# One part of four modes per weight transfer, and a 64-column block-diagonal product, in a spectral mixing kernel

## The chip, the core and the metric

The kernel runs on one core of a Trainium2 chip. The metric is device time in microseconds (us) of one execution; the numbers of the profile come from one profiled execution of its own.

## What is computed

Linear attention with the feature map elu + 1 gives `x` (8 batches, 576 positions, 512 columns). A real Fourier transform over the positions keeps 64 modes; each mode has its own complex 512 x 512 weight. The inverse transform is added to `x`, and a channel product with a rectifier follows. Cut to what matters:

```python
q_p, k_p = phi(q), phi(k)                         # phi = elu + 1
kv = einsum('bhsd,bhse->bhde', k_p, v)
x  = einsum('bhsd,bhde->bhse', q_p, kv) / (einsum('bhsd,bhd->bhs', q_p, k_p.sum(2))[..., None] + 1e-6)
X  = rfft(x, axis=1);  Xr, Xi = real(X[:, :64]), imag(X[:, :64])
Yr = einsum('bmd,mde->bme', Xr, w_r) - einsum('bmd,mde->bme', Xi, w_i)
Yi = einsum('bmd,mde->bme', Xr, w_i) + einsum('bmd,mde->bme', Xi, w_r)
u  = x + irfft(Yr + 1j * Yi)
out = u + maximum(u @ w_ch, 0)                    # float32
```

The weights `w_r` and `w_i` are 64 x 512 x 512 in float32 each, 134 MB together; a GpSimd DMA turns them into bfloat16 on the way.

## The kernel before

**Attention stage (to about 110 us).** Batch by batch: loads of q, k and v, features, the sums `kv`, the rows of `x`, the forward transform as matmuls against a table, and `place_x`, which spreads the transformed values over the 128 partitions in the order of the weights' rows (`xt_c`). The loads of the first weights are issued between (`w_next`), five pairs ahead.

**Weight stage (about 110 to 387 us).** A block `p` holds the weights of two modes, `2p` and `2p + 1`, both parts: tile `w[p]` is 128 partitions x 16 x 512. `w_load` (line 109) issues two transfers per block, one per part, each to every second partition: 64 rows of 16 KB. Five blocks are loaded ahead into five buffers; from then on two buffers turn over (`W_KEEP = 2`), so the load for block `p + 2` waits for the product of block `p`. Block 31 (`w_load_last`) comes in eight pieces, as its second mode is the last thing to arrive.

`mode_pair(p)` takes the block's weights, runs the product (line 502), copies the next block's values into a block-diagonal buffer on VectorE (`set_diagonal`, line 512), evacuates the sums (`evacuate`, on VectorE for even blocks at line 517, on ScalarE for odd ones at line 519), does pieces of other work, sums the column groups with `picks` (line 525), and does more other work. The product is 16 matmuls with 32 columns of weights (two modes, two parts, eight batches) against 512 columns of `w`; `tile_position` puts four of them on four column groups of the array. Two block-diagonal buffers `xz` take turns.

The other work (`work_slot`) is a list whose items were shared out over the blocks by hand: from block 5 on the rows of attention in float32 (lines 775 to 788, with the constant `kv_diag`, a memset at line 663), from block 15 on the fold of the early modes and the channel product (lines 802 to 852, after `YE_T`, line 550), from block 27 on the late modes (`YL`, line 635, then `z` and `yp`, lines 864 to 875, and `yb`, line 883). `keep_warm` (line 489) adds matmuls whose result nobody uses: 5 after blocks 18 to 22, 7, 10, 12 and 2 after blocks 27 to 30, and 3 inside block 30.

The last block's second mode is taken piece by piece as it lands (line 589); then come the last transposes, additions and stores (387 to 417 us).

Every engine works through its own instructions in the order of the program; `pin` keeps that order. All weight transfers are issued by GpSimd and run on one queue.

Of the kernel before, what the change touches and what calls it, by code (L numbers as in the profile page):

```python
# [20 lines left out]
def _dft_consts(S: int, NM: int):  # L21

    m = np.arange(NM)
    s_cols = np.concatenate([4 * np.arange(128) + jj for jj in range(4)] + [512 + np.arange(NP)])
    s_rows = np.concatenate([s_cols, s_cols[512:]]).reshape(5, 128).T
    ang = 2.0 * np.pi * s_rows[:, :, None] * m / S
    by_parity = np.concatenate([m[0::2], m[1::2]])
    fwd = np.concatenate([np.cos(ang)[:, :, by_parity], -np.sin(ang)[:, :, by_parity]], axis=2)

    return fwd.astype(np.float16)  # L30
# [3 lines left out]
def kernel(  # L34
# [20 lines left out]
    NMP = NM // 2  # L55
    XDC = 2 * B * NMP
# [18 lines left out]
    pick_sb = const.tile([128, 32], F16, name="pick_sb")  # L75
# [4 lines left out]

    xt_c = xpool.tile([128, NDW * XDC], BF16, name="xt_c")
    xt_v = xt_c.rearrange("p (c t b m) -> p c t b m", c=NDW, t=2, b=B)

    def xt_cols(dc: int, kk: int, n: int):

        dc = (dc // NDC * 2 + kk % 2) * NDC + dc % NDC
        c0 = dc * XDC + kk // 2
        return xt_c[:, c0 : c0 + (n - 1) * NMP + 1 : NMP]

# [14 lines left out]
    def w_load(p: int, half: int, pool, tag: str, bufs: int):  # L104
        if half == 0:
            w_in[p] = pool.tile([128, NDW, D], BF16, tag=tag, bufs=bufs, name=f"w{p}")
        two = (moe_w_r, moe_w_i)[half][2 * p : 2 * p + 2]
        pin(
            nc.gpsimd.dma_start(  # L109
                out=w_in[p][half::2], in_=two.rearrange("g (r dc) e -> (g r) dc e", dc=NDW)  # L110
            )
        )
# [24 lines left out]
    pending = [(p, half) for p in range(n_keep + n_pre) for half in range(2)]  # L137

    def w_next():
        p, half = pending.pop(0)  # L140
        pool, tag, bufs = (wpool, "w", W_KEEP) if p < n_keep else (wpre, "wp", W_PRE)
        w_load(p, half, pool, tag, bufs)
# [217 lines left out]
    place = sA.tile([128, 4, 66], BF16, name="place")  # L360
    place_l = sA.tile([128, 2, 130], BF16, name="place_l")
    nc.vector.memset(place, 0.0)
    nc.vector.memset(place_l, 0.0)

    def make_place():
        for i in range(4):
            pin(nc.vector.tensor_copy(out=place[:, i, 1:65:2], in_=id16[:, i::4]))
        for i in range(2):
            pin(nc.vector.tensor_copy(out=place_l[:, i, 1:129:2], in_=id16[:, i::2]))
        pin(nc.vector.tensor_copy(out=pick_sb, in_=id16[:, 0:32]))  # L370
        for quad in range(1, 4):
            pin(
                nc.vector.tensor_tensor(
                    out=pick_sb, in0=pick_sb, in1=id16[:, quad * 32 : quad * 32 + 32], op=ALU.add
                )
            )

# [3 lines left out]
    def place_x(b):  # L381

        x = xsp.pop(b).rearrange("p t c m -> p c t m")
        ps = psA.tile([128, 4, NDC, 2, NMP], F32, tag="big", bufs=3, name=f"xp{b}")
        for i in range(4):
            for o, ts in PARTS:
                for g in range(2):
                    pin(
                        nc.tensor.matmul(  # L389
                            ps[HALVES[g], i, :, :, 0 : NMP - 1],  # L390
                            place[:, i, 1 - o : 65 - o],
                            x[:, :, ts, g * NMP : g * NMP + NMP - 1],
                            start=(o == 0), stop=(o == 1), skip_group_check=True,
                        )
                    )
        for i in range(2):
            for g in range(2):
                for o, ts in PARTS:
                    pin(
                        nc.tensor.matmul(  # L400
                            ps[:, 2 * i + g, :, :, NMP - 1],
                            place_l[:, i, 1 - o : 129 - o],
                            x[:, :, ts, g * NMP + NMP - 1],
                            start=(o == 0), stop=(o == 1), skip_group_check=True,
                        )
                    )
        h = NDW // 2
        psf = ps.rearrange("p i c t m -> p (i c) t m")
        pin(nc.vector.tensor_copy(out=xt_v[:, 0:h, :, b, :], in_=psf[:, 0:h]))  # L409
        pin(nc.scalar.copy(out=xt_v[:, h:NDW, :, b, :], in_=psf[:, h:NDW]))  # L410
# [33 lines left out]
    for b in range(B):  # L444
        if b + 2 < B:
            load(b + 2)
            if b % 2 == 1:
                w_next()
# [29 lines left out]
    def w_get(p: int):  # L478
        if p not in w_in and p == LAST:
            w_load_last(wpool, "w", W_KEEP)  # L480
        elif p not in w_in:
            for half in range(2):
                w_load(p, half, wpool, "w", W_KEEP)
        return w_in[p]
# [13 lines left out]

    def product(P, x, n: int, w, dc: int, n_dc: int):
        c = dc % NDC * 32  # L500
        pin(
            nc.tensor.matmul(  # L502
                P[c : c + n, :], x, w[:, dc, :],
                start=(dc < NDC), stop=(dc >= n_dc - NDC), tile_position=(0, c),
                skip_group_check=True,
            )
        )

    def set_diagonal(p: int):
        for h in range(2):  # L510
            src = xt_v[HALVES[h], :, :, :, p].rearrange("p c t b -> p c (t b)")
            pin(nc.vector.tensor_copy(out=xz[p % 2][HALVES[h], :, h, :], in_=src))  # L512

    def evacuate(p: int, P):
        st = ystage.tile([128, D], F16, tag="ystage", bufs=2, name=f"ys{p}")
        if p % 2 == 0:
# [5 lines left out]
    def picks(kk: int, st, n: int):  # L522
        for ec in range(NDC):
# [4 lines left out]
                    pick_sb[:, 0 : n * 2 * B],  # L528
# [3 lines left out]
    def mode_pair(p: int):  # L532
        nonlocal yt_ps
        w = w_get(p)
        if p % 4 == 0 and p > 0:
            yt_ps = sums_bank("yt", f"yt{p // 4}", [128, NDC, 8, 2 * B], F32)
        P = psW.tile([128, D], F32, tag="P", bufs=2, name=f"P{p}")
        for dc in range(NDW):
            product(P, xz[p % 2][:, dc].rearrange("p h n -> p (h n)"), 32, w, dc, NDW)
        if p + 1 < LAST:  # L540
            set_diagonal(p + 1)
        st = evacuate(p, P)
        work_slot(p, "mid")
        if p == LAST - 1:
            keep_warm(3)
        picks(2 * p, st, 2)
# [9 lines left out]

    WARM = {2: 0, 4: 1, 6: 1, 7: 0, 8: 1}

    def last_pair():
        xl = ystage.tile([128, NDL, 2 * B], BF16, name="xl")  # L560
        for h in range(2):
            src = xt_v[:, (2 * h + 1) * NDC : (2 * h + 2) * NDC, :, :, LAST]
            pin(
                nc.vector.tensor_copy(
                    out=xl[:, h * NDC : h * NDC + NDC], in_=src.rearrange("p c t b -> p c (t b)")
                )
            )
# [4 lines left out]
        P = psW.tile([128, D], F32, tag="P", bufs=2, name=f"P{kk}")  # L572
        for dc in range(NDL):
            n = 32 if dc < NDC else 2 * B
            product(P, xt_cols(dc, kk, n), n, w, dc, NDL)
        st = evacuate(kk, P)
        work_slot(LAST, "mid")
        picks(kk, st, 1)
# [6 lines left out]
        for piece in PIECES:  # L585
            for dc in range(piece.start, piece.stop):
                for ec in range(NDC):
                    pin(
                        nc.tensor.matmul(
                            y_last[:, ec, :], w[:, NDL + dc, ec * 128 : ec * 128 + 128], xl[:, dc, :],  # L590
# [8 lines left out]
    while pending:  # L599
        w_next()  # L600
# [44 lines left out]
    xz = [ystage.tile([128, NDW, 2, 2 * B], BF16, name=f"xz{i}") for i in range(2)]  # L645
    for i in range(2):
        nc.vector.memset(xz[i], 0.0)
    set_diagonal(0)
    sums_bank = lambda tag, name, *form: psW.tile(*form, tag=tag, bufs=1, name=name)
    yt_ps = sums_bank("yt", "yt0", [128, NDC, 8, 2 * B], F32)  # L650
    z_ps = sums_bank("zl", "zl0", [128, D], F32)
    for p in range(n_early):
        mode_pair(p)
# [46 lines left out]
    def inverse_rows():  # L700
# [7 lines left out]
        for dst, src in zip(by_mode, (fwd_sb[:, 0:NJJ, :], fwd_sb[:, NJJ:, :])):  # L708
            for t in range(2):
                for o in range(2):  # L710
                    c0 = t * NM + o * NF
                    pin(
                        nc.vector.tensor_copy(
                            out=dst[:, :, 2 * o + t :: 4], in_=src[:, :, c0 : c0 + NF]
# [332 lines left out]
    for p in range(n_early, LAST):  # L1047
        mode_pair(p)
# [157 lines left out]
```

## Time and profile before

| | |
|---|---|
| Time, three runs | 418.67, 419.14, 419.21 us (median 419.14) |
| Profiled execution | 419.16 us; its span 417.2 us |
| TensorE (PE) busy | 287.5 us, 69%; mean granted clock 0.805 |
| VectorE (DVE) busy | 239.9 us, 58% |
| ScalarE (ACT) busy | 152.8 us, 37% |
| GpSimd (POOL) busy | 64.5 us, 15% |
| DMA queue of GpSimd | 81.54 MB written, 94.0% of the 16 DMA engines' span |
| HBM read | 163.66 MB |

The page cuts the span into 40 slices of 10.4 us; a digit is the busy share of a slice in tenths, and PEclk is the clock that TensorE was granted, in tenths of full speed. In a row of a group stand the line, the engine, the operation, what is written from what, the shape and the count; then busy us and mean ns of one; then the idle time of the engine just before, with what ended it. A row of the chain or the timeline begins with the start and the length in us. MB and GB/s count what is written to SBUF; for the weights twice as much is read.

### The profile page before, as it was taken

Reading aid. Unit: us, or ns where it says so; the run is one execution under the profiler, and the core shown is the slowest. Engines: PE = TensorE matmul, PEld = TensorE weight load, DVE = VectorE, ACT = ScalarE, POOL = GpSimd, SP = SyncE. Lnnn points to the kernel's source line nnn. Section 1 sums busy time; section 2 is a strip of 40 time slices with the busy share of each in tenths; the row PEclk is TensorE's granted clock in tenths of the full one; section 3 lists DMA queues with packets and bytes.
Section 4 is the critical chain, followed back from the end, with each engine's and each line's share of the span. In section 5 each row is a group of like instructions: output and inputs, shape, how many; then the busy total and the mean of one; then the engine's idle time right before and its main releaser. Section 6 shows DMA issues by size and latency. Waiting matters only on the chain.

```text
span 417.2 us, 6991 instructions
## 1 busy us (share of the span) xinstructions
PE 287.5 (69%) x2890; PEld 155.2 (37%) x2890; DVE 239.9 (58%) x534; ACT 152.8 (37%) x225; POOL 64.5 (15%) x115
## 2 busy tenths in 40 slices
PE   0279799999672454444435586977786875999993
PEld 0167677777311222212222232423332332363431
DVE  3779979994435474455535453464445452622795
ACT  4667787945110001000000243334252442241682
POOL 6232424200110111111111111111111111130200
PEclk9999958989855555666555589899898897799998
DMA  8999999999999999999999999999999999999698
GB/s 216 212 211 215 210 221 203 223 222 213 215 217 212 220 212 220 214 214 220 212 220 214 215 218 214 220 216 214 217 212 222 217 214 220 207 219 186 213 401 344
DMA packets 16996, 92.86 MB, mean 223 GB/s; under 512 B 2501, under 2 KB 3222, under 8 KB 12806
## 3 DMA queue, kind: packets, MB, share of 16 engines
q0 software_dynamic: 13088, 81.54, 94.0%
q1 hardware_dynamic: 3878, 10.90, 6.9%
q8 instruction: 22, 0.36, 0.3%
q14 instruction: 8, 0.07, 0.0%
HBM read 163.66 MB, written 9.44 MB: 415 GB/s over the span
## 4 chain that ended last, share of the span: by engine, by line
DMA 55%; PE 21%; DVE 12%; ACT 4%; issue 3%; POOL 2%; ACTq 0%; DVEq 0%; POOLq 0%
DMA w<-in_moe_w_i_dram 50%; DMA k<-in_k_dram 6%; PE P L502 6%; DVE x_main L974 4%; DVE x L298 3%; PE kvp L262 2%; PE z L864 2%; PE zl L489 2%; ACT qT L249 2%; POOL w L109 2%; PE qTp L242 1%; PE xp L389 1%; PE xf L421 1%; DVE xt_c L409 1%; PE acc L898 1%
## 5 line engine op out<-in xcount | busy, mean ns | idle before, releaser
L502 PE MATMUL P<-w,xz 128*32 128x512 bf16 x496 | 48.1, 527 | 76.6 <-DMA w<-in_moe_w_i_dram 74.4
L109 POOL DMA_DIRECT2D w<-in_moe_w_r_dram x31 | 17.4, 561 | 250.0 <-PE P L502 246.0
L519 ACT CAST ys<-P 128x512 f16<-128x512 f32 x15 | 8.8, 586 | 125.0 <-PE P L502 125.0
L502 PEld LDWEIGHTS <-xz 128*32 128x32 bf16 x496 | 13.4, 115 | 97.4 <-DMA w<-in_moe_w_i_dram 56.6
L517 DVE CAST ys<-P 128x512 f16<-128x512 f32 x17 | 11.8, 692 | 55.2 <-PE P L502 55.2
L844 PE MATMUL eps<-wch,xTw 128*128 128x512 f16 x144 | 40.6, 409 | 0.0
L827 ACT CAST x16w<-x_main 128x512 f16<-128x512 f32 x32 | 19.8, 618 | 37.3 <-DVE x_main L825 37.3
L825 DVE TENSOR_TENSOR x_main<-ya,x_main 128x512 f32<-128x512 f32 x32 | 22.0, 689 | 18.0 <-PE ya L821 17.8
L775 PE MATMUL nw<-kv_diag,qT 128*128 128x130 f16 (+1 forms) x160 | 24.3, 293 | 6.5 <-DVE x_tail L788 3.1
L262 PE MATMUL kvp<-vpad,ke 32*128 32x130 f16 x576 | 22.2, 252 | 8.3 <-ACT qT L249 8.3
L852 ACT CAST E<-eps 128x512 f16<-128x512 f32 (+1 forms) x40 | 21.2, 540 | 18.0 <-PE eps L844 17.6
L512 DVE COPY xz<-xt_c 64x256 bf16<-64x256 bf16 x62 | 22.9, 370 | 2.2 <-PE P L502 1.4
L262 PEld LDWEIGHTS <-ke 32*128 32x128 f16 x576 | 20.5, 110 | 9.7 <-issue 9.0
L298 DVE TENSOR_TENSOR x<-num,rd 128x512 f16<-128x512 f32 x32 | 22.1, 692 | 1.1
L242 PE MATMUL qTp<-id,qe 128*128 128x128 f16 x144 | 14.5, 281 | 11.6 <-DVE qe L226 9.7
L788 DVE TENSOR_TENSOR x_main<-nw,rd 128x256 f32<-128x256 f32 x32 | 11.2, 415 | 18.8 <-PE nw L775 18.8
L775 PEld LDWEIGHTS <-qT 128*128 128x128 f16 (+1 forms) x160 | 14.3, 134 | 20.0 <-issue 12.1
L836 DVE COPY xTw<-xTp 128x512 f16<-128x512 f16 x36 | 15.0, 416 | 9.8 <-PE xTp L834 9.8
L156 PE MATMUL num<-kv_sb,qT 64*128 64x65 f16 (+1 forms) x320 | 16.0, 214 | 6.3 <-DVE x L298 3.9
L249 ACT COPY qT<-qTp 128x1152 f16<-128x1152 f16 x16 | 19.6, 1290 | 1.8 <-PE qTp L242 1.5
L489 PE MATMUL zl<-wch,id 128*128 128x512 f16 x67 | 18.1, 401 | 0.0
L208 ACT ACTIVATE ke<-k 128x2304 f16<-128x2304 f16 x8 | 16.9, 2116 | 3.0 <-DMA k<-in_k_dram 2.4
(156 smaller groups left out, 520.2 us busy)
## 6 DMA issues: line engine op xcount, KB each, us to landing
w<-in_moe_w_r_dram POOLq DMA_DIRECT2D x31, 1024.0 KB, 13.1
w<-in_moe_w_i_dram POOLq DMA_DIRECT2D x31, 1024.0 KB, 17.3
out_dram<-x_main SPq DMA_DIRECT2D x14, 512.0 KB, 3.5
v<-in_v_dram POOLq DMA_DIRECT2D x8, 576.0 KB, 13.8
q<-in_q_dram POOLq DMA_DIRECT2D x7, 576.0 KB, 12.3
k<-in_k_dram POOLq DMA_DIRECT2D x6, 576.0 KB, 12.6
q<-in_q_dram SPq DMA_DIRECT2D x2, 576.0 KB, 4.5
w<-in_moe_w_r_dram POOLq DMA_DIRECT2D x2, 512.0 KB, 10.3
```

The source lines that it names most:

```text
L109: nc.gpsimd.dma_start(out=w_in[p][half::2], in_=two.rearrange("g (r dc) e -> (g r) dc e", dc=NDW))
L249: nc.scalar.copy(out=qT[:, :, c * NJ : (c + 1) * NJ], in_=qT_ps.rearrange("p j x -> p x j"))
L262: nc.tensor.matmul(kv_ps[:, h2, 0:130], phi["k", b][r0 : r0 + 32, j // NJ, j % NJ].rearrange("p o d -> p (o d)"), vp[r0 : r0 + 32, :, j, 0 ...
L298: nc.vector.tensor_tensor(out=dst.rearrange("p (o c d) -> p o c d", o=2, c=4), in0=nv[:, :, :, 0:64], in1=rden.unsqueeze(3).broadcast_to([ ...
L489: pin(nc.tensor.matmul(z_ps[:, 0:cols], id16, wch16[:, 0, 0:cols]))
L502: nc.tensor.matmul(P[c : c + n, :], x, w[:, dc, :], start=(dc < NDC), stop=(dc >= n_dc - NDC), tile_position=(0, c), skip_group_check=True,)
L512: pin(nc.vector.tensor_copy(out=xz[p % 2][HALVES[h], :, h, :], in_=src))
L775: nc.tensor.matmul(num[c][orow, h2 * 130 : h2 * 130 + 130], qT[:, c, h2, rows_of(jj, BASE[b % 2])], kv_diag[:, b, c, h2].rearrange("p o n ...
L825: pin(nc.vector.tensor_tensor(out=x, in0=acc, in1=x, op=ALU.add))
L827: pin(nc.scalar.copy(out=x16w[t], in_=x))
L844: nc.tensor.matmul(e_ps, xT[:, c, :], wch16[:, c, :], start=(c == 0), stop=(c == NDC - 1))
L852: pin(nc.scalar.copy(out=dst, in_=e_ps[:, cols]))
```

## The change

A weight transfer brings one part of four modes, not one part of two: a block `p` now holds `w_r` (even `p`) or `w_i` (odd `p`) of modes `4k` to `4k + 3`, `k = p // 2`, in 128 rows of 16 KB, with one issue per block (two pieces for block 0). Blocks 30 and 31 keep two modes with both parts. `xt` has another order, with the last mode of each quarter kept apart. The product has 64 columns of weights (four modes, two parts of x, eight batches), placed on two column groups; the two blocks of four modes add up in one PSUM tile, so there is one evacuation and one set of `picks` for every two blocks. `set_diagonal` copies 32 partitions four times and fills the buffer of block `p + 2`, the one that the product of block `p` has just read. Blocks 30 and 31 take their modes one at a time (`single`) from a small buffer `xs`, filled once. In `place_x` four 32-column placements replace pairs of 64 columns. The core of the diff:

```diff
-    def w_load(p: int, half: int, pool, tag: str, bufs: int):
-        if half == 0:
-            w_in[p] = pool.tile([128, NDW, D], BF16, tag=tag, bufs=bufs, name=f"w{p}")
-        two = (moe_w_r, moe_w_i)[half][2 * p : 2 * p + 2]
-        pin(nc.gpsimd.dma_start(out=w_in[p][half::2], in_=two.rearrange("g (r dc) e -> (g r) dc e", dc=NDW)))
+    def w_load(p: int, pool, tag: str, bufs: int, pieces_of: int = 1):
+        w = w_in[p] = pool.tile([128, NDW, D], BF16, tag=tag, bufs=bufs, name=f"w{p}")
+        m0 = 2 * (p - p % 2)
+        if p < LAST - 1:
+            four = (moe_w_r, moe_w_i)[p % 2][m0 : m0 + 4].rearrange("g (r dc) e -> (g r) dc e", dc=NDW)
+            n = 128 // pieces_of
+            for r0 in range(0, 128, n):
+                pin(nc.gpsimd.dma_start(out=w[r0 : r0 + n], in_=four[r0 : r0 + n]))
+                yield
+            return
+        for half in range(2):
+            two = (moe_w_r, moe_w_i)[half][m0 : m0 + 2]
+            pin(nc.gpsimd.dma_start(
+                out=w[half::2].rearrange("p (g dc) e -> p g dc e", g=2),
+                in_=two.rearrange("g (p dc) e -> p g dc e", dc=NDL)))
+            yield
...
-    def product(P, x, n: int, w, dc: int, n_dc: int):
-        c = dc % NDC * 32
+    def product(P, x, w, dc: int, width: int, first: bool, last: bool):
+        c = dc * width % 128
         pin(
             nc.tensor.matmul(
-                P[c : c + n, :], x, w[:, dc, :],
-                start=(dc < NDC), stop=(dc >= n_dc - NDC), tile_position=(0, c),
-                skip_group_check=True,
+                P[c : c + width, :], x, w[:, dc, :],
+                start=first, stop=last, tile_position=(0, c), skip_group_check=True,
             )
         )
 
     def set_diagonal(p: int):
-        for h in range(2):
-            src = xt_v[HALVES[h], :, :, :, p].rearrange("p c t b -> p c (t b)")
-            pin(nc.vector.tensor_copy(out=xz[p % 2][HALVES[h], :, h, :], in_=src))
+        k, part = divmod(p, 2)
+        for g in range(4):
+            rows = slice(32 * g, 32 * g + 32)
+            t0 = (1 - part) * (NQ - 1) + k
+            src = xt[rows, :, :, t0 : t0 + NQ : NQ - 1].rearrange("p b c t -> p c t b")
+            dst = xz[part][rows, :, g, :].rearrange("p c (t b) -> p c t b", t=2)
+            pin(nc.vector.tensor_copy(out=dst, in_=src))
...
-    def mode_pair(p: int):
+    def mode_block(p: int):
         nonlocal yt_ps
         w = w_get(p)
+        k, part = divmod(p, 2)
         if p % 4 == 0 and p > 0:
             yt_ps = sums_bank("yt", f"yt{p // 4}", [128, NDC, 8, 2 * B], F32)
-        P = psW.tile([128, D], F32, tag="P", bufs=2, name=f"P{p}")
+        if part == 0:
+            four_sums[:] = [new_sums(f"P{4 * k}")]
         for dc in range(NDW):
-            product(P, xz[p % 2][:, dc].rearrange("p h n -> p (h n)"), 32, w, dc, NDW)
-        if p + 1 < LAST:
-            set_diagonal(p + 1)
-        st = evacuate(p, P)
+            x = xz[part][:, dc].rearrange("p g n -> p (g n)")
+            product(four_sums[0], x, w, dc, 64, part == 0 and dc < 2, part == 1 and dc >= NDW - 2)
+        if p + 2 < LAST - 1:
+            set_diagonal(p + 2)
+        if part == 1:
+            st = evacuate(k, four_sums[0])
         work_slot(p, "mid")
-        if p == LAST - 1:
-            keep_warm(3)
-        picks(2 * p, st, 2)
+        if part == 1:
+            picks(4 * k, st, pick_sb)
...
+    def two_singles(p: int):
+        nonlocal yt_ps
+        w = w_get(p)
+        yt_ps = sums_bank("yt", f"yt{p // 4}", [128, NDC, 8, 2 * B], F32) if p % 4 == 0 else yt_ps
+        sts = [single(2 * p + g, w[:, g * NDL : g * NDL + NDL]) for g in range(2)]
+        work_slot(p, "mid")
+        keep_warm(3)
+        for g in range(2):
+            picks(2 * p + g, sts[g], pick_l)
+        work_slot(p, "end")
+        keep_warm(FILL.get(p, 0))
...
-    xz = [ystage.tile([128, NDW, 2, 2 * B], BF16, name=f"xz{i}") for i in range(2)]
+    xz = [ystage.tile([128, NDW, 4, 2 * B], BF16, name=f"xz{i}") for i in range(2)]
+    xs = ystage.tile([128, 4, NDL, 32], BF16, name="xs")
     for i in range(2):
         nc.vector.memset(xz[i], 0.0)
+    nc.vector.memset(xs, 0.0)
     set_diagonal(0)
+    set_diagonal(1)
```

The work lists, the numbers of `keep_warm` matmuls and everything after the last weights are as before.

More of the change, by code (lines that the diff above doesn't have):

```diff
@@ L135, with w_ahead @@
     nc.vector.memset(vp[:, :, :, 64:66], 1.0)
[L137 to L142, printed above, removed]
+    def w_ahead():
+        for p in range(n_keep + n_pre):
+            pool, tag, bufs = (wpool, "w", W_KEEP) if p < n_keep else (wpre, "wp", W_PRE)
+            yield from w_load(p, pool, tag, bufs, 2 if p == 0 else 1)
+    pending = w_ahead()
     def rows_of(jj: int, base: int = 0):
@@ L366, in make_place @@
         for i in range(4):
-            pin(nc.vector.tensor_copy(out=place[:, i, 1:65:2], in_=id16[:, i::4]))
+            pin(nc.vector.tensor_copy(out=place[:, i, :], in_=id16[:, i::4]))
         for i in range(2):
             pin(nc.vector.tensor_copy(out=place_l[:, i, 1:129:2], in_=id16[:, i::2]))
[L370 to L375, printed above, removed]
+        pin(
+            nc.vector.tensor_tensor(out=pick_sb, in0=id16[:, 0:64], in1=id16[:, 64:128], op=ALU.add)
+        )
+        pin(
+            nc.vector.tensor_tensor(
+                out=pick_l, in0=pick_sb[:, 0:16], in1=pick_sb[:, 32:48], op=ALU.add
             )
+        )
     xsp = {}
@@ L383, in place_x @@
         x = xsp.pop(b).rearrange("p t c m -> p c t m")
-        ps = psA.tile([128, 4, NDC, 2, NMP], F32, tag="big", bufs=3, name=f"xp{b}")
+        ps = psA.tile([128, 2, 512], F32, tag="big", bufs=3, name=f"xp{b}")
+        psv = ps[:, :, 0 : NDW // 2 * XC].rearrange("p h (i c y) -> p h i c y", i=2, c=NDC)
         for i in range(4):
-            for o, ts in PARTS:
[L387 to L394, printed above, removed]
-                    )
@@ L396, in place_x @@
[L396 to L407, printed above, removed]
@@ new lines, in place_x @@
+        for h in range(2):
+            for o, ts in PARTS:
+                pin(
+                    nc.tensor.matmul(
+                        psv[:, h, :, :, XK:].rearrange("p t c g -> p c t g"),
+                        place_l[:, h, 1 - o : 129 - o],
+                        x[:, :, ts, NQ - 1 :: NQ],
+                        start=(o == 0), stop=(o == 1), skip_group_check=True,
+                    )
+                )
+        half = NDW // 2
+        for h, copy in enumerate((nc.vector.tensor_copy, nc.scalar.copy)):
+            pin(
+                copy(
+                    out=xt[:, b, h * half : h * half + half, :],
+                    in_=psv[:, h].rearrange("p i c y -> p (i c) y"),
+                )
+            )
@@ L447 @@
             if b % 2 == 1:
-                w_next()
+                next(pending)
         turn_q(b, 0)
@@ L481, in w_get @@
         elif p not in w_in:
-            for half in range(2):
-                w_load(p, half, wpool, "w", W_KEEP)
+            for _ in w_load(p, wpool, "w", W_KEEP):
+                pass
         return w_in[p]
@@ L571, in last_pair @@
         work_slot(LAST, "start")
[L572 to L576, printed above, removed]
+        st = single(kk, w)
         work_slot(LAST, "mid")
-        picks(kk, st, 1)
+        picks(kk, st, pick_l)
         pin(nc.vector.tensor_copy(out=Y8[:, :, NA, :], in_=yt_ps[:, :, NA, :]))
@@ L597, in last_pair @@
         nc.vector.tensor_copy(out=Y8[:, :, NL - 1, :], in_=y_last)
-    while pending:
-        w_next()
+    for _ in pending:
+        pass
     tc.keep_in_program_order(
@@ L1045 @@
     )
-    for p in range(n_early, LAST):
-        mode_pair(p)
+    for p in range(n_early, LAST - 1):
+        mode_block(p)
+    two_singles(LAST - 1)
     assert not work
```

86 lines of the change are left out of this document (48 added, 38 removed).

## The prediction

> **What bounds the kernel now.** I read the page's 40 slices first, then the chain of waits, then the timeline around each `L502` product, and last the trace's own packet records.
>
> ```profile
> PEclk9999958989855555666555589899898897799998
> DMA  8999999999999999999999999999999999999698
> GB/s 216 212 211 215 210 221 203 223 222 213 215 217 212 220 212 220 214 214 220 212 220 214 215 218 214 220 216 214 217 212 222 217 214 220 207 219 186 213 401 344
> q0 software_dynamic: 13088, 81.54, 94.0%
> ```
>
> From the second slice to the 36th the 16 DMA engines are busy and move 203 to 223 GB/s. In the packet records a weight packet (16 KB in SBUF, half of what is read) takes 1.227 us, and on the same engine the next starts 19 ns before it ends. So nothing is left between packets, up to the last weight packet at 386.3 us. The change moves the same bytes: no gain larger than the gaps of this queue can come before 386 us.
>
> The chain shows the loop that feeds the queue; the numbers are start and length in us.
>
> ```profile
> 152.92 1.93 PE P L502 x16
> 154.85 0.29 issue
> 155.14 0.54 POOL w L109
> 155.68 16.61 DMA w<-in_moe_w_i_dram
> 172.33 1.92 PE P L502 x16
> ...
> 347.62 1.08 PE P L502 x16
> ...
> 350.48 1.93 PE z L864 x4
> ...
> 357.49 2.77 PE zl L489 x7
> 360.26 0.98 PE P L502 x16
> ```
>
> A product frees a buffer, GpSimd issues the transfer for two blocks later, and that waits behind the transfer already queued: 16.61 of its 19.4 us is this queue, two blocks of 9.71. From 347.6 on no DMA stands in the chain: TensorE works without a pause to the end of the weights. Two products of the timeline, one that waited and one that did not, and the last pieces:
>
> ```profile
> 230.57 1.90 PE L502 MATMUL P<-w,xz 128*32 128x512 bf16 x16 [2.17 <-DMA w<-in_moe_w_i_dram]
> 241.55 1.04 PE L502 MATMUL P<-w,xz 128*32 128x512 bf16 x8
> 377.73 1.05 PE L502 MATMUL P<-w,xz 128*32 128x512 bf16 x16
> 386.00 0.27 PEld L589 LDWEIGHTS <-w 128*128 128x128 bf16 x8 [0.19 <-DMA w<-in_moe_w_i_dram]
> ```
>
> The second is block 16, 1.27 us behind its landing (230.57 + 9.71). The fourth: TensorE reaches the last pieces only 0.2 us before they land. So there are two clocks to beat at once, the queue and TensorE's own tail.
>
> **Fewer transfers.** 29 of the 62 one-megabyte weight issues go (the built order has 81 GpSimd rows for 110). In the packet records each transfer ends in one 4-byte packet per engine that takes about 21 ns: 8 packets x 1.208 + 2 x 0.021 = 9.71, the period seen. One boundary less in each of 29 blocks is 0.6 us by the end, 0.45 of it by block 27. The 0.5 us of GpSimd per issue is not on the path: GpSimd waits 246 us for products.
>
> The Trainium skill, "DMA: Bandwidth & Descriptors", section "Anatomy of one DMA", puts a fixed cost of about 2 us on each transfer; taken as exposed time, 29 of them would be an estimated gain of 58 us. By that rule the trace disagrees: the packet records show 0.021 us per boundary, since the next transfer is always queued (what more a boundary could be worth is the rival "Faster" below).
>
> **The product.** 16 matmuls of 512 columns, four at a time, take 1.05 us at full clock and 1.90 at half: 4r + e and 8r + e, so r = 0.21 and e = 0.2. With 64 columns of weights two run at a time: 8r + e = 1.90 at full clock, 3.6 at half. The ends: 1.05 (nothing lost) and 16r + e = 3.6 (no overlap). The nearest row decides:
>
> ```profile
> L389 PE MATMUL xp<-xsp,place 128*64 128x248 bf16 x128 | 9.6, 295 | 1.0 <-ACT xsp L433 1.0
> L512 DVE COPY xz<-xt_c 64x256 bf16<-64x256 bf16 x62 | 22.9, 370 | 2.2 <-PE P L502 1.4
> ```
>
> Sixteen of these 64-column matmuls stand in the timeline with 1.07 us: pairs give 8 x 248/512 x 0.21 + 0.2 = 1.0, no overlap 1.9. I take pairs: +0.85 us a block at full clock, +1.7 at half. The Trainium skill, "TensorEngine Tiling (Array Packing)", section "Theoretical Speedup", gives 4x up to 32 columns and 2x up to 64, against this change; the trace agrees, and the sum is the same.
>
> **The diagonal.** `L512` is two copies of 0.37 us per block, made while TensorE waits for weights (one pair at 336.40, the product at 337.94). After, it is four copies of 32 partitions and as many elements: 1.5 us (ends: 0.74 if half the partitions halved the time, 3.0 if the wider stride doubled it; the row has the same element count, so 1.5). They fill the buffer that the product just read, so DVE waits for the product's end, and behind them stand the block's additions and the evacuation. Even blocks lose their evacuation (0.69 on DVE) and four picks (0.25): net on the path 0.85 + 0.8 - 0.25 = 1.4. Odd blocks pay 0.85 + 1.5, or + 2.2 where the evacuation is DVE's (blocks 4j+1); 0.3 of this hides behind the first fold matmul (0.40): 2.1 and 2.8. At half clock each is 0.85 more. The 15 evacuations and 60 picks that vanish are this credit; ScalarE is idle anyway.
>
> **Where it is covered.** TensorE's waits before the products of 143 to 231 us are 2.2 to 5.6, mean 4.3: on the whole they cover 2.3 to 3.7. A late product costs the queue only if the next transfer's first packet comes too late: product 3.6 + 0.29 + 1.6 from issue to first packet (the issue at 386.81, its packet at 388.38) = 5.5 after the start, against 9.7. So a block may be 4.2 us late at half clock, 5.9 at full.
>
> First products: the memsets double and a third comes (0.27 each for 256 words, so 1.6 for 0.55), `place_x` is shorter, the first diagonal takes 1.6 for 0.8. The first product starts at about 112.4 for 111.2 and ends at 116; the queue is full to about 123.8 (133.45 less 9.7). Covered. Then DVE waits for blocks 1, 3, 4 in turn, and the 3.5 us memset of `kv_diag` moves from 126 to about 137: block 6 is 0.7 to 3.2 late, under 4.2, and the waits take it back by block 9.
>
> Block 15 has no cover: `YE_T` now stands behind the diagonal (+0.65), the product is +1.7. Block 16 is 1.27 + 2.35 = 3.6 late. Its transfer still comes 0.6 us in time; price 0, up to 1 if I am wrong there.
>
> Blocks 16 to 26 add 6 x 1.4 + 3 x 2.8 + 2 x 2.1 = 21.0; the waits before products 17 to 27 sum to 23.6. Of the 3.6 some 1.0 to 2.6 remain: I take block 27 as 1.2 late (ends 0 and 3.6), since some of the added time falls where TensorE was waiting for DVE in any case.
>
> **The tail, the term that decides.** From product 27: three longer products, +2.55; the diagonal before `L635`, +0.6 (1.6 after the product, for 1.0); late start, +1.2; picks of block 28, -0.25; landings earlier, -0.45; the 0.2 us that TensorE had in hand. Sum +3.45. Block 30 keeps 32 columns, and its second evacuation goes to ScalarE: 0, within 0.3. Against it: from 349.7 to 359.9 the granted clock is half, three steps of 3.4 us, begun after a stretch with 62% idle. The rows it doubles (`z` 1.93 for 1.0 twice, `yp`, `yb`, `zl` 2.77 for 1.6) are worth 4.2 us. With product 27 ending near 350.4 the idle stretch moves back by about one step, so I give back one third and a little, 1.5 us. Total +1.95. After the last piece nothing changes: the 30 us of additions and stores.
>
> The profiled execution's time is 419.16 us, its span 417.2, so 2.0 lies outside; the median of the runs is 419.14, as good as the same. 419.16 + 1.95 = 421.1.
>
> **Rivals.**
> *The clock stays full (same).* For: a longer product and no wait before it leave less idle time in the stretch that brought half clock; stretches of 44% busy (336) held, 38% (346) did not. Then the whole 4.2 comes back, +3.45 turns into -0.75, and the queue's end binds at -0.6: 418.6; with half of it back 419.9. Against: TensorE still waits some 2 us for DVE's diagonal and `L635`. The Trainium skill, "TensorE: Matmul & The Clock Gate", section "Part 1: The HAM clock gate", says that a busy window of about 3.4 us brings full clock and an idle one takes it away; the trace agrees (steps of 3.41 us). 0.24.
>
> *Faster.* The queue alone decides, and the boundary is worth its whole remainder: 9.71 - 9.66 = 0.045 us over 29 blocks is 1.3, if the longer transfer loses both. With the clock full to the end, 417.9. It decides only if TensorE is in hand by more than 1 us at 386. 0.07.
>
> *The queue runs dry.* If the pairs do not overlap (product 7.0 at half clock), block 16 and those around 6 pass the 4.2 us; 3 to 5 us of empty queue and 5 more in the tail: about 428. Against: `L389`. 0.05.
>
> *The transfer is not what it says:* the built order shows one issue of 128 rows for each block from 1 to 29; block 0 in two, 30 and 31 as before. No chance of its own.
>
> **Numbers.** The measurement tells about 0.2%, 0.84 us, from no change. My forecast, a late tail with TensorE as the bound, has 0.64: 421.1, by its own bounds 420.0 to 423.9 (no clock returned and 1 us of empty queue: 3.45 + 1 = 423.6, and 0.3 for block 30). The range is 418.5 to 423.9: it takes in the full-clock case and leaves out the faster one and the dry queue. Slower is 0.64 + 0.05 = 0.69, same 0.24, faster 0.07.
>
> **What would show it.** Right: the GB/s row as now to slice 36; `L502` near 1.9 at full and 3.6 at half clock; `xz` copies that wait for PE; product 30 at about 379.7 for 377.73, and no DMA wait before the `L589` pieces. Wrong: a gap in DMA between 120 and 260 us (queue dry); a full clock through slices 34 and 35 (same); 64-column products of 1.05; or a changed length after the last piece.

## The result and the profile after

Nine runs of the changed kernel gave 420.39 to 423.49 us, median 421.63; nine of the kernel before 418.67 to 419.94, median 419.15. The ratio is 1.0059, with a 95% interval of 1.0041 to 1.0077: slower by 2.5 us. The profiled execution took 422.31 us, span 420.5 (before 419.16 and 417.2), so the trace has 3.3 us to explain, more than the median run.

The page's slices, queues and the two groups of the change:

```profile
PE 312.5 (74%) x2802; PEld 173.3 (41%) x2802; DVE 261.1 (62%) x597; ACT 148.1 (35%) x218; POOL 50.8 (12%) x86
PEclk9999855888687556866566688999999998899997
DMA  8999999999999999999999999999999999997797
GB/s 217 212 211 214 210 219 205 227 212 220 219 206 220 221 212 219 218 214 217 217 215 217 217 210 210 223 218 207 224 220 207 223 218 212 204 197 154 255 400 294
q8 instruction: 22, 0.36, 0.3%
L513 PE MATMUL P<-w,xz 128*64 128x512 bf16 x480 | 77.0, 477 | 28.3 <-DMA w<-in_moe_w_i_dram 14.9
L526 DVE COPY xz<-xt 32x256 bf16<-32x256 bf16 x120 | 45.9, 383 | 75.5 <-PE P L513 73.8
```

By the page's tenths the weight queue stays full to slice 34 as before. The product's group has grown from 48.1 to 77.0 us, the diagonal's from 22.9 to 45.9, and TensorE's idle time before products has shrunk from 76.6 to 28.3. The last slice of GB/s is new too: 294, before 344. Those are the last stores, and the prediction has no term for them.

The chain of waits, from the last product that waits for weights (start and length in us):

```profile
347.39 1.93 PE P L513 x16
...
350.52 0.38 DVE xz L526
350.92 0.77 DVE YL L665 x2
351.73 0.65 PE z L902 x2
...
353.81 1.86 PE yb L921 x4
...
357.96 2.85 PE zl L500 x7
360.81 1.85 PE P L513 x16
...
380.00 0.98 PE P L513 x16
...
387.53 0.39 PE yt L619 x16
```

In this stretch of the chain, from 347.39 to the last piece, there is no DMA; the fourth diagonal copy stands right in front of `YL`, and the product of the last pieces (`L619`) no longer waits for weights. `yb` and the fills `zl` ran at half clock. With the records of stores the span divides like this (us):

| From | Before | After | Difference |
|---|---|---|---|
| start to product 27 | 347.62 | 347.39 | -0.23 |
| to the last `Y` cast | 39.33 | 41.50 | +2.17 |
| to the end of the last addition | 25.04 | 25.04 | 0 |
| to the end of the last store's last packet | 3.91 | 5.33 | +1.42 |
| to the end of the span | 1.26 | 1.25 | -0.01 |

So the last `Y` cast is 1.94 us late, and the last store another 1.42.

### The profile page after: what moved, and what is told of

It is laid out like the page before. It is cut to its first block, busy times and chain, and to the rows that moved or that the text cites. A ratio compares the mean times of both kernels' runs of the same rounds, so it can differ in the third digit from the quotient of the medians.

```text
span 420.5 us, 6835 instructions
## 1 busy us (share of the span) xinstructions
PE 312.5 (74%) x2802; PEld 173.3 (41%) x2802; DVE 261.1 (62%) x597; ACT 148.1 (35%) x218; POOL 50.8 (12%) x86
## 4 chain that ended last, share of the span: by engine, by line
DMA 39%; PE 29%; issue 14%; DVE 13%; ACT 2%; POOL 1%; ACTq 0%; POOLq 0%
DMA w<-in_moe_w_i_dram 19%; PE P L513 11%; DMA w<-in_moe_w_r_dram 11%; DMA k<-in_k_dram 7%; DVE x_main L1012 4%; PE zl L500 3%; DVE xz L526 3%; PE eps L882 3%; DMA q<-in_q_dram 2%; PE z L902 2%; PE kvp L268 2%; PE xTp L872 1%; PE ya L859 1%; PE acc L936 1%; DVE x_main L863 1%
## 5 line engine op out<-in xcount | busy, mean ns | idle before, releaser
L513 PE MATMUL P<-w,xz 128*64 128x512 bf16 x480 | 77.0, 477 | 28.3 <-DMA w<-in_moe_w_i_dram 14.9
L526 DVE COPY xz<-xt 32x256 bf16<-32x256 bf16 x120 | 45.9, 383 | 75.5 <-PE P L513 73.8
L513 PEld LDWEIGHTS <-xz 128*64 128x64 bf16 x480 | 36.1, 132 | 61.2 <-issue 50.5
L533 ACT CAST ys<-P 128x512 f16<-128x512 f32 x8 | 4.7, 586 | 121.4 <-PE P L513 121.4
L106 POOL DMA_DIRECT2D w<-in_moe_w_i_dram x15 | 9.4, 624 | 154.6 <-PE P L513 145.9
L248 PE MATMUL qTp<-id,qe 128*128 128x128 f16 x144 | 16.8, 310 | 12.0 <-DVE qe L232 9.7
L106 POOL DMA_DIRECT2D w<-in_moe_w_r_dram x16 | 9.9, 620 | 105.2 <-PE P L513 86.1
L872 PE MATMUL xTp<-id,x16w 128*128 128x128 f16 x144 | 14.9, 229 | 8.2 <-ACT x16w L865 8.2
L248 PEld LDWEIGHTS <-qe 128*128 128x128 f16 x144 | 14.6, 145 | 13.1 <-DVE qe L232 10.1
L882 PEld LDWEIGHTS <-xTw 128*128 128x128 f16 x144 | 12.7, 101 | 13.1 <-DVE xTw L874 3.3
```

The costliest lines, as they stand in the source:

```text
L248: nc.tensor.transpose(qT_ps[:, j], phi["q", b][:, c, j].rearrange("p o d -> p (o d)"), id16,)
L513: nc.tensor.matmul(P[c : c + width, :], x, w[:, dc, :], start=first, stop=last, tile_position=(0, c), skip_group_check=True,)
L526: pin(nc.vector.tensor_copy(out=dst, in_=src))
L882: nc.tensor.matmul(e_ps, xT[:, c, :], wch16[:, c, :], start=(c == 0), stop=(c == NDC - 1))
```

## Experiments

The ratio is to runs of the kernel before that were made beside the experiment (median 418.96 to 419.08), with its 95% interval. Experiments 1 to 4, 5 to 8 and 9 to 12 ran on three chips, and the changed kernel itself was not run again beside them; so the distance of an experiment's time from its 421.63 is less sure than the ratio. Each experiment has one profiled execution, and what is said of causes holds for that one. Theory T is the prediction's: TensorE's own chain sets the tail. A second theory, F, came out of the first four profiles.

### What makes the tail longer

**1. Only the width, in the kernel before.**

```diff
-        for dc in range(NDW):
-            product(P, xz[p % 2][:, dc].rearrange("p h n -> p (h n)"), 32, w, dc, NDW)
+        for _ in range(2 if p in (27, 28, 29) else 1):
+            for dc in range(NDW):
+                product(P, xz[p % 2][:, dc].rearrange("p h n -> p (h n)"), 32, w, dc, NDW)
```

> The kernel before, with the sixteen matmuls of products 27, 28 and 29 issued twice (the second pass starts the sums anew), so that each of these three lasts as long as the changed kernel's product and nothing else differs. Theory T (TensorE's own chain from product 27 to the last piece sets the end): three times 0.85 us, less 0.2 in hand and less what the clock gives back (0 to 1.5): 420.0 to 421.5. Rival Q (the weight queue's form and its end decide, TensorE's length does not): 419.0 to 419.4.

Measured 420.69 us, ratio 1.0051 (1.0036 to 1.0066). The number fits T; the profile does not. The last `Y` cast is at 387.15, only 0.2 later than before: the clock stayed full from 347 to 367, TensorE had time in hand, and the pieces wait for weights again. The other 1.3 us lie behind the last addition, as in the changed kernel. T gave the right time for a wrong reason.

**2. The changed kernel without the width.**

```diff
-            x = xz[part][:, dc].rearrange("p g n -> p (g n)")
-            product(four_sums[0], x, w, dc, 64, part == 0 and dc < 2, part == 1 and dc >= NDW - 2)
+            x = xz[part][:, dc, 0:2].rearrange("p g n -> p (g n)")
+            product(four_sums[0], x, w, dc, 32, part == 0 and dc < 4, part == 1 and dc >= NDW - 4)
```

> The changed kernel, but each product of blocks 0 to 29 uses 32 of its 64 columns (it leaves out two of each four modes), four matmuls at a time again. Transfers, diagonal copies, evacuations and picks stay as changed. Theory T: the products fall back to about 1.05 us, the tail gets 2.6 us shorter and the last weights bind again: 418.5 to 419.7. Rival Q: 421.6 as the changed kernel. Rival D (the four diagonal copies ahead of the additions are the cost): 420.6 or more.

Measured 420.00, ratio 1.0031 (1.0021 to 1.0042). Product 27 starts at 347.17 and the last weights end at 385.81, 0.45 and 0.47 us earlier than in the profile before: that is what the merged transfers give. The last `Y` cast is at 386.58, also earlier. Yet the time is 1 us longer than before, all of it behind the last addition. The four copies are in this kernel too, so rival D falls for the tail.

**3. The diagonal behind the additions.**

```diff
-        if p + 2 < LAST - 1:
-            set_diagonal(p + 2)
         if part == 1:
             st = evacuate(k, four_sums[0])
...
                 late_modes(g, yt_ps)
+        if p + 2 < LAST - 1:
+            set_diagonal(p + 2)
         work_slot(p, "end")
```

> The changed kernel, with the four diagonal copies of a block moved behind its evacuation and behind the copy of the finished sums (L665), which come first on VectorE. Theory T, in which the copies in front of L665 put 1.25 us into the tail at block 27: 420.2 to 420.9, less still if the clock gets its cold window back out of the shorter idle time. If only the width of the products counts: 421.6 as the changed kernel. Rival Q: 421.6.

Measured 424.25, ratio 1.0117 (1.0103 to 1.0132): all theories missed. Ahead of product 15 the copies now stand in front of VectorE's additions to `x_main`, for which TensorE waits 1.84 us, and product 15 starts at 231.47 for 230.51 in the changed kernel. Behind it `YE_T` follows sooner, but the copies stand in front of `ye_slots`: TensorE's wait there grew from 0.51 to 1.18 us. Product 16 starts at 244.46 for 243.25, and the queue runs empty behind it (below). The copies were only moved to another waiter.

**4. Fewer fills in the tail.**

```diff
-    FILL = {**{p: 5 for p in range(18, 23)}, 27: 7, 28: 10, 29: 12, 30: 2}
+    FILL = {**{p: 5 for p in range(18, 23)}, 27: 7, 28: 4, 29: 6, 30: 2}
```

> The changed kernel, with 12 of the 22 filling matmuls behind blocks 28 and 29 taken out (10 and 12 become 4 and 6), 2.6 us of TensorE time that computes nothing. Theory T: product 30 at 377.3 instead of 379.9, the last pieces reach their weights before they land, and a DMA wait stands in front of them; the end is then the last weights': 419.3 if they land at 386.3 as before the change, 420.8 if they land at 387.4 as in the changed kernel's profile. Rival Q with TensorE out of it: 421.6.

Measured 424.25, ratio 1.0134 (1.0116 to 1.0152). The tail did what T says: product 30 waits 2.87 us for weights, and from product 27 to the last `Y` cast it takes 40.43 us instead of 41.50. But product 27 itself is at 348.74, 1.35 late. The edit lies behind block 28, so this loss cannot come from it. It comes from block 16, where this execution had half clock to 246.5 us, the changed kernel's to 244.5. The other four runs (424.07 to 426.34) have no trace, so what made them long stays open. Timelines of the changed kernel (first two lines) and of this one:

```profile
243.59 2.34 PE L513 MATMUL P<-w,xz 128*64 128x512 bf16 x15
246.24 0.64 POOL L106 DMA_DIRECT2D w<-in_moe_w_r_dram  x1 [11.16 <-PE P L513]
```

```profile
244.19 3.04 PE L513 MATMUL P<-w,xz 128*64 128x512 bf16 x15
247.54 0.63 POOL L106 DMA_DIRECT2D w<-in_moe_w_r_dram  x1 [11.92 <-PE P L513]
```

The issue behind product 16 came at 246.24, 247.54 and (experiment 3) 248.13. It is for block 18. In the packet records that block's last packet ended 9.77, 11.46 and 11.84 us after block 17's, where 9.7 is the full queue. At 246.24 the first engines stood idle (first engine to first engine 11.07 us), but the engines finished block 17 2.5 us apart and the later ones lost next to nothing. In experiments 4 and 3 the issue came 1.3 and 1.9 us later and the engines were only 1.5 apart: there the last engine lost 1.8 and 2.2 us.

### What makes the last store late

In the profiles of the changed kernel and of experiments 1 to 4 the last store's last packet comes 5.2 to 5.4 us behind the last addition, but 3.9 in the profile before. The packet records show one difference. Queue `q8` fetches instructions, 16 KB in a packet of about 0.93 us; by the spacing they are TensorE's, one packet for some 125 matmuls with their weight loads. In the kernel before the last fetch is at 390.2 us, ahead of the dense stores. In the others it falls between 404.8 and 411.8, while all 16 engines write at 400 GB/s together, and then the last ten or so store packets, about one engine's share, end one after the other over some 1.4 us in which all other store packets have ended. The change takes 88 matmuls out of TensorE's program (2890 to 2802), and so moves every fetch. This is theory F.

**5. The kernel before with a longer program.**

```diff
             fold_table()
+            pad_ps = psA.tile([128, 2, 512], F32, tag="big", bufs=3, name="pad")
+            for _ in range(36):
+                pin(nc.tensor.matmul(pad_ps[0:64, 0, 0:16], id16[:, 0:64], id16[:, 0:16]))
         sum_kv(b)
```

> The kernel before with 36 narrow matmuls (64x16 each, into a PSUM tile that nobody reads) added at 13 us, where TensorE waits 7.9 us for ScalarE. Their only lasting effect is that TensorE's program is 72 instructions longer ahead of the end. Theory F (the 16 KB instruction fetches of queue q8 come at fixed places of TensorE's program, every 125 or so matmuls with their weight loads, and one that falls into the full store stream delays the last store): the last fetch moves from 390.2 us to about 405 to 409 and the time becomes 420.2 to 420.6, with the last x_main addition where it was (410.8). Rival (the 1.3 us between the last addition and the end of the span belong to something else of the changed kernel): 418.8 to 419.3.

Measured 420.48, ratio 1.0038 (1.0024 to 1.0052). The matmuls ran at 21.1 us and not at 13, for 2 us, but nothing of that was left at product 27 (347.43, before 347.62). From the page and from VectorE's timeline, with the last addition of the kernel before in the last line:

```profile
PE 288.5 (69%) x2926; PEld 155.6 (37%) x2926; DVE 240.1 (57%) x534; ACT 152.8 (37%) x225; POOL 64.3 (15%) x115
GB/s 214 212 211 215 210 221 203 219 223 219 212 216 210 221 219 212 218 217 216 218 208 223 219 210 219 208 222 220 208 223 216 213 218 212 220 211 173 257 400 297
q8 instruction: 23, 0.38, 0.3%
410.54 1.22 DVE L977 TENSOR_TENSOR x_main<-acc,x_main 128x1024 f32<-128x1024 f32 x1
410.77 1.22 DVE L974 TENSOR_TENSOR x_main<-acc,x_main 128x1024 f32<-128x1024 f32 x1
```

The last addition is 0.23 us earlier than before, there is one fetch more, at 406.9, the last slice falls from 344 to 297 GB/s, and the last store lands 5.20 us behind the addition. F is shown: 36 matmuls that nobody uses, far from the end, cost 1.3 us at the end.

**6. The changed kernel with the old program length, at the same place.** The edit is that of experiment 5, with 90 matmuls.

> The changed kernel with 90 such narrow matmuls at the same place, so that its TensorE program is about as long as before. Theory F: the last fetch moves from 409.2 to about 392, where the store stream is not yet full, and the time falls by 1.3 to 1.4, to 420.0 to 420.5. Rival: 421.3 to 421.9 as the changed kernel.

Measured 424.13, ratio 1.0106 (1.0089 to 1.0123). The last fetch is at 393.6 and the last store lands 3.86 us behind the addition, as F says; but the total missed: here too the matmuls did not run at 13 us but from 21.0, and these 90 pushed the first stage back by 4.9 us, of which 2.7 were left at product 27.

**9. The same, hidden in waits.**

```diff
         keep_warm(FILL.get(p, 0))
+        keep_warm(22 if p in (23, 24, 25, 26) else 0, 16)
```

> The changed kernel with 22 narrow matmuls (128x16, 0.06 us each) behind each of blocks 23 to 26, where TensorE waits 1.3 to 2.3 us for weights: 88 in all, the same lengthening of TensorE's program as the 90 at 13 us, without their delay at the start. Theory F: the last fetch moves from 409.2 to about 393, the last store lands about 3.9 us behind the last addition instead of 5.3, and the time falls by 1.3 to 1.4, to 420.0 to 420.6. If F is only a part of the delay of the last store: 420.7 to 421.3. If F is wrong: 421.6.

Measured 420.62, ratio 1.0059 (1.0031 to 1.0088). The profiled execution took 419.17, with the last fetch at 390.1; the page's row shows the end as before the change:

```profile
GB/s 216 212 211 214 208 217 205 223 220 217 216 214 214 220 215 217 215 215 218 215 217 218 216 212 210 220 221 207 222 217 213 223 206 225 216 210 190 209 402 346
```

Half of the twelve runs lie between 419.17 and 419.98, the other half between 421.27 and 425.41. So the mechanism of F is taken out (3.86 us again), and the fastest run is 1.2 us below the changed kernel's fastest (420.39), but the ratio is no better than the changed kernel's. It may be that the narrow matmuls fill waits that covered TensorE's other delays; the long runs have no trace, so this is not shown. What F costs in the median is shown by experiment 5 for the kernel before, 1.4 us; for the changed kernel it is carried over from the packet records and not shown by this total.

| Kernel (profiled execution) | Last fetch | Last addition's end to last store's end |
|---|---|---|
| before; 6; 9; 10; 11; 12 | 388.9 to 393.6 | 3.8 to 3.9 us |
| after; 1; 2; 3; 4; 5; 7; 8 | 404.8 to 411.8 | 5.2 to 5.4 us |

Why 0.93 us of fetch cost 1.4 was not settled. Nor is an early fetch always free. In experiment 11 it falls at 391.07, beside the small transfers from `last_z` to `YZ_all`. Their last packet ends 6.55 us behind the start of the last `Y` cast, in the other profiles 5.25 to 5.66; TensorE waits for them, and the last addition ends 26.34 us behind that start, elsewhere 25.04 to 25.12. That the fetch is the cause is likely from the place and the size, but no run tests it.

### Versions that take the costs out

**7. Half of the diagonal to ScalarE.**

```diff
-            set_diagonal(p + 2)
+            set_diagonal(p + 2, (0, 1))
         if part == 1:
             st = evacuate(k, four_sums[0])
+        if p + 2 < LAST - 1:
+            set_diagonal(p + 2, (2, 3), nc.scalar.copy)
```

> The changed kernel with two of a block's four diagonal copies moved from VectorE to ScalarE, behind the evacuation that ScalarE makes. Theory T (copies in front of L665, YE_T and the evacuations stand in TensorE's way): block 16 0.7 us and the tail 0.7 us earlier, and the queue is not empty behind block 16; the fetch of F stays: 420.3 to 421.0. If the copies cost nothing: 421.6.

Measured 420.64, ratio 1.0052 (1.0028 to 1.0076). Block 16 starts at 242.55, 0.7 earlier as expected. But half clock lasts to 245.1, its product ends at 245.88 (245.93 in the changed kernel), and the queue still runs empty: block 18's last packet ends 10.69 us after block 17's, against the forecast. The profile has the wide products and still the old tail: 39.33 us from product 27 to the last `Y` cast. Its timeline:

```profile
351.59 1.31 PE L904 MATMUL z<-wch,YL 128*128 128x512 f16 x4 [0.85 <-DVE YL L667]
353.67 1.02 PE L923 MATMUL yb<-YZ_all,inv_sb 64*128 64x512 f16 x4 [0.52 <-DVE YZ_all L915]
356.00 1.67 PE L500 MATMUL zl<-wch,id 128*128 128x512 f16 x7
357.61 1.92 PE L513 MATMUL P<-w,xz 128*64 128x512 bf16 x16
385.57 0.36 PE L621 MATMUL yt<-xs,w 128*128 128x16 bf16 x8 [0.21 <-DMA w<-in_moe_w_i_dram]
```

TensorE waits 0.85 for `YL` (1.46 in the changed kernel), its clock is full (`yb` 1.02 for 1.86, `zl` 1.67 for 3.05), product 28 starts 3.1 us earlier, and the pieces wait for weights. What is left over the kernel before is F and 0.2 us. This does not show that the moved copies gave the tail back: experiment 8, with all four copies on VectorE, has the same full clock and a tail of 39.31.

**8. Less work between products 15 and 16.**

```diff
-        [((first_fold, "end"), 5)]
+        [((first_fold, "end"), 3)]
```

> The changed kernel with less of the fold work between products 15 and 16 (three items in place of five; the rest goes behind products 16 to 26). Theory M (the queue runs empty behind block 16 when its product is late, by more where the steps of the clock fall badly, 0.2 to 1.3 us): product 16 at 241.5 instead of 243.3, no empty queue, 420.6 to 421.3 and less spread between runs. Rival (TensorE's tail and F alone make the difference): 421.6.

Measured 422.41 (420.41 to 423.38), ratio 1.0068 (1.0047 to 1.0089). In the profiled execution, one of 420.41, M's steps are there: product 16 at 241.19 and no empty queue. The time and its spread are not what M said; the other five runs have no trace, so what made them longer stays open.

**10. Experiment 7 with the narrow matmuls of 9.**

> The kernel with the split diagonal copies (two on VectorE, two on ScalarE) and the same 88 narrow matmuls. Theory T and F together: the last weights bind the tail as in the profile of the split kernel (last Y cast 387.2), the last store lands 3.9 us behind the last addition: 419.0 to 419.6, so level with the kernel before. If only one of the two is real: 420.2 to 420.8.

Measured 420.00 (418.56 to 424.38), ratio 1.0025 (1.0003 to 1.0047): between the two forecasts. The profiled execution had half clock in the tail again, and the tail took 40.70 us with the last store 3.8 behind the last addition.

**11. The same with four fills fewer in the tail** (28: 8, 29: 10, and 23 narrow matmuls for 22).

> As the one with split copies and narrow matmuls, with two of the filling matmuls fewer behind block 28 and two behind block 29 (8 and 10 for 10 and 12; 0.9 us), and 92 narrow ones for 88 so that the program keeps its length. Theory T: where the clock of the tail is half for two steps, the 0.9 us comes back; where it is full, the weights bind anyway: 418.9 to 419.5, with fewer long runs. If the fills are needed to keep the clock: 419.5 to 421.

Measured 419.40, ratio 1.0014 (0.9996 to 1.0033), in T's range. The profiled execution (420.22) had full clock in the tail, where T expects nothing from fewer fills, so the trace does not show that they brought the gain.

**12. And four fold items between products 15 and 16** (the weight 5 of experiment 8 becomes 4).

> The same with four fold items in place of five between products 15 and 16. Theory M: product 16 about 0.9 us earlier, no empty queue behind it: 418.7 to 419.3. If the empty queue no longer matters with the split copies: as the kernel without this edit.

Measured 419.23 (418.48 to 421.87), ratio 1.0012 (0.9997 to 1.0026): not to be told from the kernel before. Experiments 10 to 12 went down step by step, though neighbours overlap in their intervals. No version beats the kernel before.

## Why the prediction came out right, and where it was wrong

The range holds the result, 421.63 for a forecast of 421.1, and in the profile the mechanism is the one forecast: TensorE's own chain, and no longer the weights, sets the last `Y` cast. That the number is so close is in part luck. In the profiled execution the last `Y` cast is 1.94 us late, where the sum had 1.95, because two of its terms miss by about the same and cancel. Product 27 was to start 0.75 us later (1.2 of lateness less 0.45 of earlier landings) and starts 0.23 earlier; the clock was to give back 1.5 us and gives back 0.70. Behind that cast come 1.42 us at the stores, for which the sum had nothing. So the profiled execution, 422.31, lies 1.2 above the forecast, and the median 0.5.

**Right, to a tenth.** The product takes 1.92 us at full and 3.62 at half clock (1.90 and 3.6 forecast), so pairs of 64 columns overlap, as the row `L389` had it. (The Trainium skill says so too, "TensorEngine Tiling (Array Packing)", section "Theoretical Speedup", with 2x for 64 columns.) A diagonal copy of 32 partitions takes 0.383 (0.37). In the tail the three products cost 2.61 (2.55), the diagonal in front of `L665` 0.61 (0.6), block 30 starts at 379.93 (379.7), and the weights no longer bind the last pieces. The queue gains no more from 29 fewer transfers than the boundaries that were counted: 0.45 us at product 27 in experiment 2, as forecast. In the changed kernel itself product 27 is only 0.23 early.

**The first blocks.** Product 0 came at 113.9 us (112.4 forecast) and was covered: product 5 waits for its weights and starts at 133.42, before at 133.50. Not block 6 but block 8 came late, and block 9 waits again.

**Block 16.** Forecast 3.6 us late at a price of 0, up to 1. It is 3.0 late (243.25 for a landing at about 240.2), and in the profile the price is under 0.1. In experiments 3 and 4 it is 1.8 to 2.2, so the bound was too small for kernels like this one: part of the margin is the spread of the DMA engines, which differs between executions, and a product at half clock for longer uses it up. Nor is the spread a sure margin: in experiment 7, with the issue as early as in the changed kernel (246.18), the last engine still lost 1.0.

**Block 27, the step that failed in the sum.** "I take block 27 as 1.2 late." It is not late: TensorE waits for weights before each product from 23 on, 1.34 us before product 27. The net costs per block of 1.4 to 2.8 were too high: from product 16 to product 27 TensorE's time without its waits for weights grew from 82.5 to 96.6 us, by 14.2 and not by 21.0. And part of the lateness was counted twice. The 23.6 us of waits are those of a trace in which product 16 was already 1.27 late, so they had to cover only the 2.35 that came on top, and 2.35 + 21.0 is below 23.6: by its own figures the sum had no lateness at product 27.

**The clock.** Forecast 1.5 us back. Between the first `z` and product 28 the changed kernel gives back 0.70. Here the size missed, and the certainty too: half clock in this stretch is not a property of the kernel. (In the rival on the clock, half of 4.2 back gives 420.5 by the prediction's own sum, not 419.9.) Mean granted clock between 347 and 357 and between 357 and 367 us, and the tail from product 27 to the last `Y` cast:

| Products | Kernel: clock, clock | Tail, us |
|---|---|---|
| 32 columns | before: 0.63, 0.85; experiment 2: 0.62, 0.87; 5: 0.78, 0.88 | 39.3 to 39.4 |
| 64 columns (or twice 32) | 1, 7, 8, 11, 12: 1.00, 1.00 | 39.3 to 39.6 |
| 64 columns | after: 0.84, 0.82; 10: 0.80, 0.86; 3: 0.96, 0.69; 6: 0.98, 0.68 | 40.7 to 41.7 |

(9 lies between: 0.86, 0.97 and 39.9; 4 waits for block 30's weights, 40.4.) In these profiles neither the width nor the half clock lengthens the tail alone. Together they do, because the weights then stop being the last to come. The rival "the clock stays full" is thus not excluded by the result: experiment 8, whose code behind block 27 is that of the changed kernel, had its tail, though not its 418.6: its profiled execution took 420.41, as the late fetch stays.

**"After the last piece nothing changes", the step that was missing.** Engine work behind it is equal to 0.01 us, but the last store is not: +1.42. A changed length after the last piece was one of the prediction's own signs of being wrong. The forecast counted the matmuls that vanish only as time, not as a shift of the instruction fetches. The chain of waits does not show it either, since it ends at the last addition.

So I read the 2.5 us of the median as 1.3 to 1.4 of F, which should be in every run, as the program's length is, less the 0.23 of the queue; the rest I put to the tail at half clock and the empty queue behind block 16, in some runs and not in others. The first part fits the fastest of the nine runs, 420.39, which is 1.24 above the median of before. The division is argued and not shown: only one of the nine runs has a trace.

## What to carry to other kernels

Merging transfers in a queue that never runs empty is worth only its boundaries (here 0.02 us each); what it costs elsewhere, a wider product and copies that wait for it, decides, and the copies must be weighed by who stands behind them. Where two resources end within a microsecond of each other, ask of a longer step not only what it adds but whether it and the clock together pass the other resource, and expect the answer to differ from run to run. Before a difference of 0.3% is put down to an edit, compare the last store with the last instruction: a change of program length anywhere can move an instruction fetch into the final stores.

## What was not expected of the hardware

- TensorE's instructions come in 16 KB packets of 0.93 us, beside the data. One of them in a store stream of 400 GB/s made the last store 1.4 us late; at 389 to 394 us, ahead of that stream, it did not delay the last store.
- The 16 DMA engines work through one queue up to 2.8 us apart (3.4 in the profile before), and this spread can hide a short gap: 1.4 us of empty queue for the first engine cost the last one less than 0.1. In experiment 7 it did not: 1.0 us for the first cost the last 1.0.
- A GpSimd issue for 128 rows takes 0.62 us, one for 64 rows 0.56 (means of the groups); half as many issues take a little over half the time.
